# Diagonal score tiles packed by quarters, nine exponential fills per unit in place of ten, and keys turned from a buffer

## The chip, the cores and the metric

The kernel runs on one core of a Trainium2 chip. The core has a matrix engine (TensorE, PE in the profile), whose weight loads are listed apart as PEld, a vector engine (VectorE, DVE), an engine for activation functions (ScalarE, ACT), GpSimd (POOL) and SyncE (SP), which here issues nearly all DMAs. The metric is device time in microseconds (us); the median of several timed executions counts.

## The reference

The output has two halves side by side, 640 columns each, for 2048 tokens.

Half A is a convolution over the whole sequence. Keys are filtered with four short taps per channel, multiplied by the values, convolved with a filter of 2048 taps per channel (an FFT in the reference), and multiplied by the queries:

```
kv = k_shift * v
y  = irfft(rfft(kv padded) * rfft(ssm_k padded))[:2048] + kv * ssm_D
a  = q * y
```

Half B is attention with 32 heads of 20 channels, in four segments of 512 tokens. In a segment each token attends causally to tokens of the same segment (softmax), and to earlier segments through a memory matrix that is summed up from segment to segment:

```
p     = softmax(q k^T * scale + mask);  a_dot = p v
a_mem = phi(q) M / (phi(q) z + 1e-6)
o     = g * a_mem + (1 - g) * a_dot;  b = o wo
M    += phi(k)^T v;  z += sum phi(k);   phi(t) = t + 1 where t > 0, else exp(t)
```

## The kernel before

Half A is cut into five blocks of 128 channels (`conv(dp)`, dp 0 to 4). The long convolution is a transform done by matmuls with a constant matrix (`spectrum`), a product of spectra on VectorE (`product`), and matmuls back (`inverse`). The short filter (`short_filter`) is done by matmuls, too: the keys lie turned, channels on partitions, in `kr`, each eighth token is taken as weights, and diagonal matrices of taps (`skd`) are streamed through. For dp in `TAP2` (2, 3 and 4) pairs of taps are joined: half of the partitions hold keys shifted by two tokens, copied by three DMAs between `kr` and `kb`, so that fewer columns are streamed. The keys come to `kr` by one transposing DMA from memory.

Half B has eight units: four segments, each with two halves of 16 heads (`project(u)` and `attend(u)`, u from 0 to 7). `project` multiplies the segment's turned input `xT` by the weights, evicts keys, queries and values to SBUF, turns keys and queries by DMA into `KQT`, takes the positive feature map (`phi`), bounds the scores (`bound`, whose rows are written into spare rows of the turned queries by four small DMAs), and adds this segment to the memory `Mbd`.

`attend` treats the 16 heads in four groups of four. A head has 20 channels on 32 partitions, so the four heads of a group lie on the four quarters of the array's rows, and their matmuls stand side by side. Scores are made transposed: keys on partitions, queries along the columns. A segment of 512 tokens has four token tiles of 128; of the 4 x 4 blocks of scores the ten at and below the diagonal are needed. They are put into *fills*. A fill is four PSUM banks, one per head, of 512 columns each, and two exponentials (ACT, 128 x 1024 each) that carry it to an SBUF buffer `ET`. Per group there is one fill A (keys of tile 0 with queries of tiles 1 to 3, and keys of tile 2 with queries of tile 3) and one fill D (the four diagonal blocks). Per two groups there is one fill J (keys of tile 1 with queries of tiles 2 and 3, for both groups). This makes ten fills and twenty exponentials per unit. In a fill D the mask is put into PSUM first: 16 matmuls of constant matrices (`pack` in the profile), then 16 of keys and queries.

`values` then multiplies the exponentials, as weights, by the values with a column of ones (21 columns), 40 matmuls per group, and beside them four matmuls with the memory for later segments. VectorE takes reciprocals, scales, adds the two parts and writes `o_s`. `project_out` turns `o_s` and multiplies it by `wo`.

All operations are recorded first (`Recorder`), and a list of numbers worked out beforehand (`ORDER`) says in which order they are issued, engine by engine; another (`BASE`) gives each group of results its PSUM banks. So all instructions carry the line of the issuing helper, L256, and the profile is read by tiles and shapes. The string `EVICT` says for each of 238 evictions whether VectorE (1) or ScalarE (0) does it. SP's queue is served in order: a DMA whose source is not ready holds up those behind it. Warming matmuls (`WARM`, tile `o` in the profile) run at the start.

## Time and profile before

| What | Value |
|---|---|
| Median of three timed runs | 272.57 us (272.38 to 272.6) |
| Profiled execution: span from the first to the last instruction | 272.0 us |
| Time outside that span, median less span | about 0.6 us |
| PE busy, instructions | 260.8 us, 4368 |
| PE weight loads busy, instructions | 195.4 us, 4371 |
| DVE busy, instructions | 250.9 us, 424 |
| ACT busy, instructions | 248.8 us, 388 |
| DMA, queue of SP | 42.91 MB, 79.9% of 16 engines' time |

The profiled execution's own time was not taken apart from its span; the timed median stands beside it. The table's busy times are unions: where two instructions of an engine overlap, the time counts once. PE instructions are listed with a modelled end and overlap strongly, so for PE the distance between starts is what an instruction costs. A shape like `32*128 32x384` means weights of 32 rows by 128 columns, and an input of 32 rows by 384 columns streamed through them. In a row of groups the numbers are: busy us, mean ns of one, idle time before them and who ended it. A row of the timeline has start, length, engine, operation, shapes and count of instructions that follow each other; a row of waits has total us, times, longest.

### The profile page before, as it was taken

To read this page: it belongs to the slowest core of one execution; us is meant where nothing else is said; L and a number is where in the kernel's file an instruction comes from. 1 tells how busy PE (TensorE), PEld (TensorE's weight loads), DVE (VectorE), ACT (ScalarE), POOL (GpSimd) and SP (SyncE) were. 2 spreads that over 40 slices of the span, in tenths; PEclk is the share of its full clock that TensorE was granted. 3 is DMA by queue.
4 is the path that set the end of the run, shared out by engine and by line. 5 is a ranking of instruction groups with operands and counts; after the bars stand their busy time and mean duration, and the time that the engine had idled before them with its cause. 6 is when DMAs were issued, how large, how long until landed. Compare 5 with 4: busy or idle time off the path is not lost.

```text
span 272.0 us, 10130 instructions
## 1 busy us (share of the span) xinstructions
PE 260.8 (96%) x4368; PEld 195.4 (72%) x4371; DVE 250.9 (92%) x424; ACT 248.8 (91%) x388; POOL 6.9 (3%) x18
## 2 busy tenths in 40 slices
PE   8999999999998999999999999999999989999995
PEld 3879777868766677878676787768677765756783
DVE  0599999999999999999999999999999998999972
ACT  1586799999999999999999999999999998999962
POOL 9100000000000000000000000000000000000000
PEclk9999999999999999999999999999999997999999
DMA  6999399999989599998979599994974081894024
GB/s 166 347 207 243 82 191 225 311 194 172 170 217 201 144 195 195 191 178 159 159 165 190 116 151 226 147 197 65 146 177 82 4 154 27 169 155 90 27 68 133
DMA packets 126972, 43.74 MB, mean 161 GB/s; under 512 B 117339, under 2 KB 124512, under 8 KB 126800
## 3 DMA queue, kind: packets, MB, share of 16 engines
q1 hardware_dynamic: 126768, 42.91, 79.9%
q8 instruction: 34, 0.56, 0.9%
q0 software_dynamic: 160, 0.20, 0.2%
q14 instruction: 10, 0.08, 0.1%
HBM read 14.12 MB, written 7.34 MB: 79 GB/s over the span
## 4 chain that ended last, share of the span: by engine, by line
PE 55%; ACT 33%; issue 6%; DVE 4%; ACTq 0%; DVEq 0%
PE ps L256 55%; ACT ET L256 21%; ACT F L256 4%; ACT KQ L256 3%; ACT PP L256 3%; ACT outb L256 1%; ACT Va L256 1%; DVE F L256 1%; DVE pq L256 1%; DVE Kh L256 1%; ACT bT L256 1%; DVE qabs L256 0%; DVE vt L256 0%; DVE Xh L256 0%; DVE PP L256 0%
## 5 line engine op out<-in xcount | busy, mean ns | idle before, releaser
L256 ACT ACTIVATE ET<-ps 128x1024 bf16<-128x1024 f32 x160 | 160.6, 1102 | 1.9 <-PE ps L256 1.7
L256 PE MATMUL ps<-wqkv,xT 128*128 128x320 bf16 x480 | 76.3, 300 | 0.5 <-ACT ET L256 0.3
L256 PEld LDWEIGHTS <-xT 128*128 128x128 bf16 x640 | 58.1, 98 | 25.7 <-issue 5.2
L256 PE MATMUL ps<-Va,ET 128*128 128x21 bf16 x1280 | 42.4, 172 | 0.3 <-ACT ET L256 0.3
L256 ACT CAST F<-ps 128x512 bf16<-128x512 f32 x69 | 42.0, 687 | 0.3 <-PE ps L256 0.3
L256 PEld LDWEIGHTS <-ET 128*128 128x128 bf16 x1280 | 39.7, 96 | 3.0 <-issue 2.2
L256 PE MATMUL ps<-KQT 32*128 32x128 bf16 (+2 forms) x896 | 34.6, 240 | 1.1 <-ACT ET L256 1.0
L256 PEld LDWEIGHTS <-Wf 128*128 128x128 bf16 x320 | 28.9, 97 | 6.1 <-issue 1.5
L256 ACT CAST KQ<-ps 128x320 bf16<-128x320 f32 x61 | 28.2, 496 | 1.4 <-PE ps L256 1.3
L256 PE MATMUL ps<-wo,xT 128*128 128x320 bf16 x160 | 25.4, 299 | 0.0
L256 PEld LDWEIGHTS <-KQT 32*128 32x128 bf16 x896 | 16.0, 92 | 10.9 <-issue 9.9
L256 PE MATMUL ps<-vt,Wf 128*128 128x256 bf16 x160 | 22.4, 272 | 0.1
L256 PE MATMUL ps<-kT,Wf 128*128 128x256 bf16 x160 | 22.2, 273 | 0.2 <-ACT ET L256 0.2
L256 PE MATMUL ps<-Y,Wi 128*128 128x256 bf16 x160 | 21.7, 280 | 0.0
L256 DVE TENSOR_TENSOR o<-ps,rr 128x640 bf16<-128x640 f32 x24 | 19.5, 814 | 0.2
L256 PE MATMUL ps<-Mbd,PqT 128*128 128x84 bf16 x96 | 18.1, 202 | 1.2 <-ACT ET L256 0.9
L256 DVE TENSOR_TENSOR Y<-Y,pq 128x2048 bf16<-128x2048 bf16 (+1 forms) x20 | 18.6, 945 | 0.0
L256 DVE TENSOR_TENSOR pq<-Xh,Kh 128x2048 bf16<-128x2048 bf16 x15 | 18.1, 1209 | 0.0
L256 PEld LDWEIGHTS <-Wi 128*128 128x128 bf16 x160 | 15.3, 100 | 3.5 <-issue 1.0
L256 ACT ACTIVATE PP<-KQ 128x640 bf16<-128x640 bf16 (+1 forms) x18 | 17.7, 991 | 0.0
L256 PE MATMUL ps<-pack 32*128 32x128 bf16 x512 | 14.7, 216 | 1.9 <-ACT ET L256 1.7
L256 ACT CAST Va<-ps 128x320 bf16<-128x320 f32 x31 | 15.0, 520 | 1.2 <-PE ps L256 1.2
(93 smaller groups left out, 370.0 us busy)
## 6 DMA issues: line engine op xcount, KB each, us to landing
vt<-in_A_v_dram SPq DMA_DIRECT2D x10, 256.0 KB
pq<-in_A_q_dram SPq DMA_DIRECT2D x10, 256.0 KB
out_dram<-outb SPq DMA_DIRECT2D x13, 160.0 KB
turned<-kT SPq DMA_DIRECT2D x4, 512.0 KB
kT<-turned SPq DMA_DIRECT2D x8, 256.0 KB
out_dram<-pq SPq DMA_DIRECT2D x8, 256.0 KB
kb<-kr SPq DMA_DIRECT2D x6, 256.0 KB
Wf<-c_wf SPq DMA_DIRECT2D x4, 256.0 KB
```

Of the source, the lines that this page charges most:

```text
L256: f(*[fix(a) for a in args], **{k: fix(v) for k, v in kw.items()})
```

## The change

The diagonal blocks are packed closer. Of a diagonal block of 128 x 128 one quarter (later keys, earlier queries) is masked altogether, so three quarters of it are kept. Token tiles 2 and 3 are held with their halves of 64 tokens exchanged, from the load of `x` on (five transposing DMAs in place of one, and an exchanged identity in segment 0), until the output is written (two stores of 64 rows in place of one for tiles 2 and 3) or turned back in the last segment. With that, the small quarter (64 keys, 64 queries) of a tile 2 or 3 lies on partitions 64 to 127 and that of tile 0 or 1 on partitions 0 to 63, and a pair of diagonal blocks takes 192 columns instead of 256. Two pairs take 384, and the 128 columns left in a fill D take the block of keys 1 and queries 2. What was left in J (keys 1, queries 3) is one block per group, and one J per unit holds it for all four groups, in a buffer of its own (`EJ`). So a unit has four fills A, four D and one J.

In a D fill there are now 24 mask matmuls of 64 columns; sixteen score matmuls of 64 columns with 128-column weights, sixteen with 64-column weights that go to one half of the partitions, and four of 128 columns, in two rounds of the loop over `P`. The diagonal's value matmuls become an operation of its own (`OD`): per group 16 matmuls with weights of 64 rows by 128 columns, then 16 with 64 rows by 64 columns, the two of a pair on opposite rows and into different banks. The other 24 value matmuls per group stay. In segment 0 the two groups of a pair share one set of banks and one division.

Beside that: the keys of dp 1 to 4 are loaded in token rows into `kb` (two DMAs), turned from there into `kr` (two transposing DMAs) so that the tokens taken together lie side by side, and copied by five DMAs; dp 1 joins those with paired taps. The tap matrices of dp 0 and 1 are made at the start (`filter_weights`). The memory's old state is added in PSUM by a matmul with the identity, where two VectorE steps did it before. `phi` of the queries is done once for four token tiles, not twice for two. The column of ones stands ahead of the values in place of behind them, with a second one for the memory. `A` of the bounds has 4 columns in place of 32. There are 10 warming matmuls for 20, six `ET` buffers for seven, a new `ORDER` and `BASE`, and an `EVICT` with 26 ones of 238 in place of 31. `KSW` and `IW` are all 1, so they join nothing.

```diff
+    def filter_weights(self, dp):
+        V = self.nc.vector
+        self.rec.key = ("skd", dp)
+        if dp in TAP2:
+            w = self.ring("skd", [128, 2, 2, 64], n=1)
+            V.tensor_tensor(out=w[:], in0=self.id2[:, None, None, :].to_broadcast([128, 2, 2, 64]),
+                            in1=self.taps[:, 0:4, dp].rearrange("p (f l) -> p f l", f=2)[:, :, :, None].to_broadcast([128, 2, 2, 64]), op=ALU.mult)
+        else:
+            w = self.ring("pq", [128, 4, 4, 128], n=PQBUF)[:, 0]
+            V.tensor_tensor(out=w, in0=self.ident[:, None, :].to_broadcast([128, 4, 128]), in1=self.taps[:, 4:8, dp, None].to_broadcast([128, 4, 128]), op=ALU.mult)
+        self.skd[dp] = w
...
+                    rows = flat[:, 1024 * a:1024 * a + 1024]
+                    nc.sync.dma_start(out=rows.rearrange("p (e d) -> p e d", e=8), in_=self.k[1024 * a:1024 * a + 1024, dsl].rearrange("(p e) d -> p e d", e=8))
+                for a in range(2):
+                    key("kx", a)
+                    nc.sync.dma_start_transpose(out=kr[:, :, KPAD + 128 * a:KPAD + 128 * a + 128], in_=flat[:, 1024 * a:1024 * a + 1024])
                 key("lc")
                 q = self.queue("lc", dp)
-                q.dma_start(out=self.kb[64:128, KPAD:KPAD + S], in_=kr[64:128, KPAD:KPAD + S])
-                q.dma_start(out=self.kb[0:64, KPAD:KPAD + S], in_=kr[64:128, KPAD - 2:KPAD + S - 2])
-                q.dma_start(out=kr[64:128, KPAD:KPAD + S], in_=kr[0:64, KPAD - 2:KPAD + S - 2])
+                q.dma_start(out=kb[64:128], in_=kr[64:128])
+                q.dma_start(out=kb[0:64, 2:8], in_=kr[64:128, 0:6])
+                q.dma_start(out=kb[0:64, 0:2, KPAD - 1:], in_=kr[64:128, 6:8, KPAD - 2:-1])
+                q.dma_start(out=kr[64:128, 2:8], in_=kr[0:64, 0:6])
+                q.dma_start(out=kr[64:128, 0:2, KPAD:], in_=kr[0:64, 6:8, KPAD - 1:-1])
+            else:
+                nc.sync.dma_start_transpose(out=flat[:, KPAD:KPAD + S], in_=self.k[:, dsl])
...
-            nc.sync.dma_start_transpose(out=xT[:], in_=self.x[L * s:L * s + L, :])
+            for to, n, at in ((0, 256, 0), (256, 64, 320), (320, 64, 256), (384, 64, 448), (448, 64, 384)):
+                nc.sync.dma_start_transpose(out=xT[:, :, to:to + n], in_=self.x[L * s + at:L * s + at + n, :])
...
+                        nc.tensor.matmul(pmv[:, k, :, 1:VW], lhsT=PP[:, 0, t, 4 * k:4 * k + 4, :], rhs=Va[:, t, 4 * k:4 * k + 4, 1:VW],
+                                         start=(k == 0 and t == 0), stop=False, grp=g, skip_group_check=True)
+                nc.tensor.matmul(pmv[:, :, :, 1:VW], lhsT=self.ident[:], rhs=src[:, :, :, 1:VW], start=False, stop=True, grp=g, skip_group_check=True)
+            V.tensor_tensor(out=dst[:, :, :, 1:VW], in0=pmv[:, :, :, 1:VW], in1=self.maskbd[:, None, :, 1:VW].to_broadcast([128, 4, 4, DH + 1]), op=ALU.mult, grp=g)
...
+            ET = self.ring("EJ", [128, 4, 4, 128])[:].rearrange("p h g q -> p h (g q)") if kind == "J" else self.ring("ET", [128, 4, 512], n=ETBUF)
...
         def diagonal(gg):
+
             def parts(heads):
-                for i in range(4):
-                    for hl, bank, r, g in heads:
-                        nc.tensor.matmul(bank.rearrange("p (b q) -> p b q", b=4)[:, :, 32 * i:32 * i + 32], lhsT=self.mleft[r, i, :],
-                                         rhs=self.mright[r, None, :].to_broadcast([32, 4, 32]), start=(i == 0), stop=False, grp=g, skip_group_check=True)
-                for kc in range(4):
-                    for hl, bank, r, g in heads:
-                        block(bank[:, 128 * kc:128 * kc + 128], hl, gg, kc, 128 * kc, 128, start=False, stop=(kc == 3), grp=g)
+                for i in range(2):
+                    for at, m0 in ((64, 64), (128, 0), (0, 128)):
+                        for hl, bank, r, g in heads:
+                            nc.tensor.matmul(bank[:, 0:384].rearrange("p (b q) -> p b q", b=2)[:, :, at + 32 * i:at + 32 * i + 32], lhsT=self.mleft[r, i, m0:m0 + 128],
+                                             rhs=self.mright[r, None, :].to_broadcast([32, 2, 32]), start=(i == 0 and at == 64), stop=False, grp=g, skip_group_check=True)
+                for P in range(2):
+                    a, b = 128 * P, 128 * P + 256
+                    for at, k, q in ((128, a, a + 64), (0, b, b)):
+                        for hl, bank, r, g in heads:
+                            nc.tensor.matmul(bank[:, 192 * P + at:192 * P + at + 64], lhsT=KT[r, gg, k:k + 128], rhs=QT[r, gg, q:q + 64], start=False, stop=False, grp=g, skip_group_check=True)
+                    for to, k, q in ((0, a, a), (64, b + 64, b + 64)):
+                        for hl, bank, r, g in heads:
+                            nc.tensor.matmul(bank[to:to + 64, 192 * P + 64:192 * P + 128], lhsT=KT[r, gg, k:k + 64], rhs=QT[r, gg, q:q + 64], start=False, stop=False, grp=g, skip_group_check=True)
+                for hl, bank, r, g in heads:
+                    block(bank[:, 384:512], hl, gg, 1, 256, 128, start=False, stop=True, grp=g)
             return parts
...
-        def joined(g0):
-            def parts(heads):
-                for k in range(2):
-                    for hl, bank, r, g in heads:
-                        block(bank[:, 256 * k:256 * k + 256], hl, g0 + k, 1, 256, 256, start=True, stop=True, grp=g)
-            return parts
...
+        def joined(heads):
+            for k in range(4):
+                for hl, bank, r, g in heads:
+                    block(bank[:, 128 * k:128 * k + 128], hl, k, 1, 384, 128, start=True, stop=True, grp=g)
+
+        def weighted(gg, Dg, Bg, J, g, j):
+            if s:
+                sums = g.ap[:, :, 0:352].rearrange("p b (k c h e) -> p b k c h e", k=2, c=2, h=4)
+                dots, mems = sums[:, :, 0], sums[:, :, 1]
+            else:
+                dots = g.ap[:, :, 0:352].rearrange("p b (c k h e) -> p b c k h e", k=2, c=2, h=4)[:, :, :, j]
+            up, low = slice(0, 64), slice(64, 128)
+            rec.key = ("OD", u, gg)
+            with rec.one():
+                for late in range(2):
+                    for P in range(2):
+                        a, b = 192 * P + 64, 192 * P
+                        for hl in range(4):
+                            if late:
+                                todo = [(0, low, low, Dg[low, hl, a + 64:a + 128]), (1, up, up, Dg[up, hl, b:b + 64])]
+                            else:
+                                todo = [(0, up, slice(0, 128), Dg[up, hl, a:a + 128]), (1, low, slice(0, 128), Dg[low, hl, b:b + 128])]
+                            for odd, rows, to, e in todo:
+                                nc.tensor.matmul(dots[to, odd, P, hl, 0:DH + 1], lhsT=e, rhs=Va[rows, P + 2 * odd, 4 * gg + hl, 0:DH + 1],
+                                                 start=(not late and P == 0 and hl == 0 and j == 0), stop=False, grp=g, skip_group_check=True)
...
+                        for q in (0, 1) if qc == 1 else (qc,):
+                            nc.tensor.matmul(mems[:, q // 2, q % 2, :, 1:VW], lhsT=PqT[:, q, gg, :], rhs=Mbd[:, gg, :, 1:VW], start=False, stop=False, grp=g, skip_group_check=True)
                     for hl in range(4):
+                        blocks = [(0, Bg[:, hl, 128 * (qc - 1):128 * qc])]
+                        blocks += [(1, Dg[:, hl, 384:512] if qc == 2 else J[:, hl, 128 * gg:128 * gg + 128])] if qc > 1 else []
+                        blocks += [(2, Bg[:, hl, 384:512])] if qc > 2 else []
+                        for kc, e in blocks:
+                            nc.tensor.matmul(dots[:, qc // 2, qc % 2, hl, 0:DH + 1], lhsT=e, rhs=Va[:, kc, 4 * gg + hl, 0:DH + 1], start=False, stop=True, grp=g, skip_group_check=True)
...
+        J = fill("J", ("J",), joined)
         for pp in range(2):
             g0 = 2 * pp
-            A0 = fill("A", (g0, "A"), 235, below(g0))
-            D0 = fill("D", (g0, "D"), 456, diagonal(g0))
-            J = fill("J", (g0, "J"), 235, joined(g0))
-            A1 = fill("A", (g0 + 1, "A"), 235, below(g0 + 1))
-            D1 = fill("D", (g0 + 1, "D"), 456, diagonal(g0 + 1))
-            values(g0, D0, A0, J)
-            values(g0 + 1, D1, A1, J)
+            parts = []
+            for gg in (g0, g0 + 1):
+                Dg = fill("D", (gg, "D"), diagonal(gg))
+                Bg = fill("A", (gg, "A"), below(gg))
+                parts.append((Dg, Bg))
+            values(pp, parts)
...
-FBUF, ETBUF, PQBUF = 1, 7, 1
-WARM, WARMC = 20, 512
+FBUF, ETBUF, PQBUF = 1, 6, 1
+WARM, WARMC = 10, 512
...
-TAP2 = (2, 3, 4)
+TAP2 = (1, 2, 3, 4)
...
```

More of the change, by code (lines that the diff above doesn't have):

```diff
@@ L280, in __init__ @@
         self.real = tc.nc
[L281 removed]
+        self.rings, self.skd = {}, {}
         self.evicts = 0
@@ L344, in __init__ @@
         self.evict(self.taps[:], tp, g)
+        for dp in range(2):
+            self.filter_weights(dp)
         rec.key = ("zero",)
@@ L643, in project @@
             tok = slice(128 * t, 128 * t + 128)
+            rows = [xT[:, cc, tok] for cc in range(5)]
             rec.key = ("P", u, t)
@@ L649, in project @@
                         for cc in range(5):
-                            nc.tensor.matmul(g.ap[:, i, 0:320], lhsT=xT[:, cc, tok], rhs=self.wqkv[:, cc, half, i0 + i, :], start=(cc == 0), stop=(cc == 4), grp=g)
+                            nc.tensor.matmul(g.ap[:, i, 0:320], lhsT=rows[cc], rhs=self.wqkv[:, cc, half, i0 + i, :], start=(cc == 0), stop=(cc == 4), grp=g)
                 self.evict(KQ[:, t, i0:i0 + KQW, :, 0:DH], g.ap[:, :, 0:320].rearrange("p i (h d) -> p i h d", d=DH), g)
@@ L849, in project_out @@
             rec.key = ("OB", s, t)
-            self.stores(last).dma_start(out=self.out[L * s + 128 * t:L * s + 128 * t + 128, D:2 * D], in_=outb.rearrange("p a b -> p (a b)"))
-FBUF, ETBUF, PQBUF = 1, 7, 1
-WARM, WARMC = 20, 512
+            rows = self.out[L * s + 128 * t:L * s + 128 * t + 128, D:2 * D]
+            flat = outb.rearrange("p a b -> p (a b)")
+            for x, y in ((0, 64), (64, 0)) if t > 1 and not last else ((0, 0),):
+                n = 128 if x == y else 64
+                self.stores(last).dma_start(out=rows[x:x + n], in_=flat[y:y + n])
+FBUF, ETBUF, PQBUF = 1, 6, 1
+WARM, WARMC = 10, 512
 TURN = (0,)
```

245 lines of the change are left out of this document (114 added, 131 removed).

## The prediction

> **What bounds the kernel now.** I read the page first, then the groups of instructions with shapes kept apart, then the timeline of TensorE (PE) and last the waits.
>
> ```profile
> span 272.0 us, 10130 instructions
> PE 260.8 (96%) x4368; PEld 195.4 (72%) x4371; DVE 250.9 (92%) x424; ACT 248.8 (91%) x388; POOL 6.9 (3%) x18
> PE 55%; ACT 33%; issue 6%; DVE 4%; ACTq 0%; DVEq 0%
> PE ps L256 <- ACT ET L256: 5.2, 15, 0.7
> ```
>
> Three engines are busy over 90% of the span, and the chain of waits runs through PE for 55% and ACT for 33%. Matmuls overlap, so 260.8 says little of what PE has left. The distance from one start to the next says it. The fence holds rows of PE's timeline: start, length, shape, count.
>
> ```profile
> 42.66 1.10 PE L256 MATMUL ps<-skd,kr 128*128 128x512 bf16 x7
> 43.60 1.52 PE L256 MATMUL ps<-wqkv,xT 128*128 128x320 bf16 x10
> ...
> 116.27 0.39 PE L256 MATMUL ps<-ident,kmx 128*128 128x128 bf16 x4
> 116.59 0.40 PE L256 MATMUL ps<-pack 32*128 32x128 bf16 x16
> 116.82 0.39 PE L256 MATMUL ps<-KQT 32*128 32x128 bf16 x16
> 117.15 0.28 PE L256 MATMUL ps<-skd,kr 128*128 128x128 bf16 x1
> ...
> 120.54 0.85 PE L256 MATMUL ps<-wqkv,xT 128*128 128x320 bf16 x5
> 121.32 0.40 PE L256 MATMUL ps<-KQT 32*128 32x384 bf16 x8
> 121.65 0.85 PE L256 MATMUL ps<-wqkv,xT 128*128 128x320 bf16 x5
> 122.34 0.22 PE L256 MATMUL ps<-skd,kr 128*128 128x128 bf16 x1
> ...
> 122.93 0.84 PE L256 MATMUL ps<-wqkv,xT 128*128 128x320 bf16 x5
> ...
> 125.67 1.04 PE L256 MATMUL ps<-vt,Wf 128*128 128x256 bf16 x8
> 126.54 0.20 PE L256 MATMUL ps<-Mbd,PqT 128*128 128x84 bf16 x1
> 126.58 0.25 PE L256 MATMUL ps<-Va,ET 128*128 128x21 bf16 x4
> ...
> 127.30 0.55 PE L256 MATMUL ps<-Va,ET 128*128 128x21 bf16 x16
> 127.71 0.20 PE L256 MATMUL ps<-Mbd,PqT 128*128 128x84 bf16 x1
> ```
>
> Five projections take 122.34 - 121.65 = 0.69 when another 128-row matmul follows, 0.137 each, but 121.32 - 120.54 = 0.78 when a 32-row fill follows: going to 32 rows costs 0.10. Fill A (8 matmuls, four heads side by side, 512 columns a head) holds PE for 0.33, of which 512/320 x 0.137 = 0.22 is streaming, so the way back costs 0.11. Fill D takes 0.23 for masks, 0.33 for scores, 0.10 to enter: 0.66. A round of four heads with 128 columns is 0.23/4 = 0.057. Sixteen value matmuls take 127.71 - 127.30 = 0.41, 0.026 each; eight of 256 columns 0.87, 0.109 each; an 84-column one 0.04. One convolution tile takes 0.94 with full taps (dp 0 and 1), 122.93 - 122.34 = 0.59 with paired taps.
>
> Counts come from the groups, two of which stand here, and from the loops of the code (160 output projections, three times 160 matmuls of 256 columns, 80 fills, 32 of them D). PE's work without waits:
>
> ```profile
> L256 PE MATMUL ps<-wqkv,xT 128*128 128x320 bf16 x480 | 76.3, 300 | 0.5 <-ACT ET L256 0.3
> L256 PE MATMUL ps<-Va,ET 128*128 128x21 bf16 x1280 | 42.4, 172 | 0.3 <-ACT ET L256 0.3
> ```
>
> (480 + 160) x 0.137 = 87.7; 1280 x 0.026 = 32.8; 480 of 256 columns x 0.109 = 52.3; 48 fills A and J x 0.43 = 20.6; 32 fills D x 0.66 = 21.1; 192 of 84 columns x 0.04 = 7.7; convolution 8 x 0.94 + 12 x 0.59 = 14.6; 120 turning matmuls x 0.057 = 6.8; bounds 8 x 0.44 = 3.5; warming about 7. Together 254. PE starts at 1.3 and 3.4 us pass after its last matmul, so of 272.0 only some 13 us are waits, 5.2 of them for the exponentials. **PE's own work is a bound, as tight as ACT and DVE.**
>
> **The change, part by part.** The sum is against the span of 272.0; the timed median of 272.57 lies 0.6 above it.
>
> ACT. Nine fills of two exponentials in each of 8 units are 144 for 160.
>
> ```profile
> 227.45 5.61 ACT L256 ACTIVATE ET<-ps 128x1024 bf16<-128x1024 f32 x6 [1.34 <-PE ps L256]
> L256 ACT ACTIVATE ET<-ps 128x1024 bf16<-128x1024 f32 x160 | 160.6, 1102 | 1.9 <-PE ps L256 1.7
> L256 ACT CAST KQ<-ps 128x320 bf16<-128x320 f32 x61 | 28.2, 496 | 1.4 <-PE ps L256 1.3
> L256 DVE TENSOR_TENSOR mt<-mt,em 128x16 bf16<-128x16 bf16 x6 | 1.3, 212 | 0.0
> L256 DVE TENSOR_TENSOR Mbd<-Mbd,mt 128x336 bf16<-128x336 bf16 x6 | 2.0, 325 | 0.0
> L256 DVE TENSOR_TENSOR PP<-PP,qabs 128x640 bf16<-128x640 bf16 x12 | 5.7, 474 | 0.0
> L256 DVE TENSOR_TENSOR PP<-PP,qabs 128x1280 bf16<-128x1280 bf16 x6 | 4.9, 816 | 0.0
> ```
>
> Six in a row step by (5.61 - 1.10)/5 = 0.90, so 16 fewer free 14.4 us. The string of evictions has 26 on DVE for 31: five go to ACT, at most 0.5 each, 2 us. With the merged phi (half as many, twice as long, some 1 us less) ACT falls by 13 to 236.
>
> DVE loses those five (about 2.5), the two memory steps at 0.212 and 0.325 six times (3.2), half the phi steps (5.7 to 4.9, and as much again for its companion, 1.6), and a little where segment 0 treats two head groups in one step (1): some 8 us, to 243.
>
> PE, the fills. J goes from 16 to 8, each still 0.43 (four rounds of 0.057, 0.10 in, 0.11 out): -3.4. D becomes six mask rounds of 64 columns, four score rounds of 64 columns into 128 partitions, four into 64 partitions, one of 128 columns. No row shows 32-row rounds of 64 columns; half of 0.057 is the floor, 0.029, and 0.057 the ceiling. I take 0.029, since value matmuls of 21 columns reach 0.026 with a full weight load each. The rounds into 64 partitions have one relative in the trace, the filter's turning at the start. It loads 64 columns of weights into the two halves in turn and then 128 columns. The rows come from short stretches of the timeline, one ending just after the first pair, one after the fourth, one further on; the last row is of the groups:
>
> ```profile
> 9.19 0.22 PE L256 MATMUL ps<-ident,skd 5*64 5x5 bf16 x2
> ...
> 9.19 0.40 PE L256 MATMUL ps<-ident,skd 5*64 5x5 bf16 x8
> ...
> 9.53 0.25 PE L256 MATMUL ps<-ident,skd 5*128 5x5 bf16 x3
> L256 PE MATMUL ps<-ident,skd 5*64 5x5 bf16 x8 | 0.4, 201 | 0.0
> ```
>
> From two matmuls to eight the group grows by 0.18: pairs follow each other every 0.06, though they stream five columns. The last pair starts near 9.59 - 0.20 = 9.39 and the first 128-column one at 9.53: 0.13, about 0.10 beyond the floor of 0.026. **So going from 64 to 128 columns of the array costs what going to 32 rows does.** D's loop over the two pairs of tiles goes to 64 and back twice, four switches of 0.10 inside each fill. D is then 0.10 + 10 x 0.029 + 2 x 0.06 (the rounds for both halves together) + 4 x 0.10 + 0.057 + 0.11 = 1.08, 0.42 more, 32 times: +13.4. If the switches cost nothing it is +0.6; with rounds at 0.057 it is +22.
>
> The Trainium skill, TensorEngine Tiling (Array Packing), Key Properties, says that changing the tiling mode, not only the tile, drains TensorE; the 0.10 and 0.11 of the fills agree, and the sum by the rule is the one above.
>
> PE, the values. The sixteen diagonal matmuls of a head group (0.41) become 32: eight pairs on 64 rows, then eight pairs on 64 rows and 64 columns. The two of a pair use other rows and other banks, so I count a pair once: 8 x 0.026 for the first set, and for the second between 0.026 (a value matmul) and 0.06 (the turning above, whose weights were read in strides). I take the middle, 0.043. Three switches (into 64 rows, to 64 columns, back) add 0.30. That is 0.84, 0.43 more, 32 times: +13.8, with ends +9 and +18. Where the new order puts the set next to a fill one switch is shared; I take that everywhere, -3.2.
>
> On the weights' price the Trainium skill, TensorE: Matmul & The Clock Gate, Weight-path perf modes, says that the fast load needs 128 columns. With its plain rate, columns over 1.2 per ns, 64 columns are an estimated 53 ns and the sum is 2.6 us more.
>
> PE, the rest. dp 1 goes to paired taps, 4 x (0.94 - 0.59) = -1.4; keys that lie in a row instead of every eighth should load at the streaming pace, 6 x 0.057 + 4 x 0.029 = 0.46 for 0.59 on 16 tiles, -2.1 (0 if strides were not the cause). The memory's sum by an identity matmul of 336 columns is 6 x 0.14 = +0.8. Ten warming matmuls fewer save nothing, as PE then waits for the same first load:
>
> ```profile
> 1.26 6.16 PE L256 MATMUL ps<-o 128*128 128x512 bf16 x18 [1.26 <-DVE o L256]
> ...
> 7.25 0.66 PE L256 MATMUL ps<-ident,kT 128*128 128x128 bf16 x8
> ```
>
> Net for PE: -3.4 + 13.4 + 13.8 - 3.2 - 3.5 + 0.8 = +18.
>
> Queues. Each paired dp turns its keys from the buffer kb: two loads, two transposes and five copies where dp 2 to 4 had one transpose and three copies.
>
> ```profile
> 81.63 3.42 SPq L256 DMA_TRANSPOSE kr<-in_A_k_dram  x1
> 94.75 1.39 SPq L256 DMA_TRANSPOSE KQT<-KQ  x1
> 97.48 1.31 SPq L256 DMA_DIRECT2D kb<-kr  x2
> SPq L256 <- PE ps L256: 45.1, 19, 9.2
> ```
>
> At 1.39 a transpose of 256 KB and 0.65 a copy that is 7.3 us of issue for 5.4, and 7.3 for 3.4 on dp 1; twelve more transposes of x in small pieces (same bytes) and six more stores add under 10. Behind them in SP's queue stand the turned KQ and the bound rows, for which the fills wait. SP now waits 45.1 us for PE alone, so some 20 us more of issue fit; bounds 0 and +5, taken 0.
>
> Buffers. D and B of a pair of head groups hold four of six buffers until their values ran, and J has its own, so a third pair's fill can start; before, two pairs shared seven. I take 0; if a fill had to wait for values, a round of 0.8 each would be the price of one wait.
>
> **Sum.** PE 254 + 18 = 272 of work, 4.7 at the two ends, and 3 of the 13 us of waits: those for ACT and DVE shrink, as both now have 25 us to spare, those for the first loads stay. Span 279.6, time 280. With 13 us of waits 290, with the cheap values and no waits 272.
>
> **The rivals.**
> Faster, by relief of ACT and DVE: the 64-wide tiles run beside the 128-wide ones without a drain. Then D costs +0.6, the values 0, and PE falls by 6 to 248. DVE decides: 243 of work and the 21 us in which it was not busy (272.0 - 250.9) give 264; between 260 and 269 with the sharing of evictions. For it speaks that PE waits for ACT, 5.2 us; against it the 0.13 at 9.4 us. It decides if D fills come out under 0.75 and the value sets near 0.45.
> No change: value sets at the cheap end (+9), nothing waits any more; 267 + 4.7 = 272.
> Much slower: rounds of 64 columns held at 0.057 by weight loads (+9) and SP's longer queue bringing keys or rows late (+5): 290 to 298. Each of 72 fills would start late after a transpose.
> That fewer exponentials run is fixed by the counts, so the change does at least that.
>
> **How the numbers follow.** Forecast 280 (274 to 290) 0.49; faster, 264, 0.33; no change 0.10, split 0.04, 0.05, 0.01; much slower 0.08. A measurement here can tell 0.2%, 0.5 us. Faster 0.37, same 0.05, slower 0.58. The range 262 to 290 leaves out under 2 in 10: the lower half of the fast case and most of the slowest.
>
> **What would show it.** Right: D fills near 1.1 from first mask to next start, 0.13 gaps between 64- and 128-column rounds, value sets near 0.8, PE without waits while ACT and DVE show holes, exponentials x144. Wrong: 64-column rounds 0.03 after 128-column ones, ACT and DVE still full at a shorter span; or SP's transposes ending the waits of fills.

## The result, and the profile after

The changed kernel takes 305.19 us (median of four runs, 301.92 to 305.9) where the kernel before takes 272.56. By the means of the runs that is 1.117 times as long, with a 95% interval of 1.111 to 1.123. The forecast was 280, range 262 to 290; the direction was right and the size was not. Medians here leave out a run more than 1.5% above the fastest of its kernel (there is one each in `keys_before`, `regroup`, `before_narrow`, `lean_replan2` and `after_pool`), while the expectations' gains of 2.8 us for `keys_before` and 4.8 for `regroup` have it counted. The profiled execution, the slowest of the four, shows a span of 304.1 us. From its page come the span, the busy times, the granted clock in 40 slices and the chain by engine:

```profile
span 304.1 us, 12942 instructions
PE 281.7 (93%) x5786; PEld 207.9 (68%) x5787; DVE 249.9 (82%) x385; ACT 242.4 (80%) x371; POOL 7.2 (2%) x18
...
PEclk9999997999999599999999999999599999979999
...
PE 58%; DMA 17%; SPq 11%; DVE 6%; ACT 3%; issue 3%; DVEq 0%; ACTq 0%
```

Two numbers divide the 32.1 us of span. PE is busy 281.7 us for 260.8 (+20.9), and the time in which it is not busy goes from 272.0 - 260.8 = 11.2 to 304.1 - 281.7 = 22.4 us (+11.2). The chain of waits, in which ACT had 33% before, now has 28% of DMAs and SP's queue, and ACT 3%.

The relief of ScalarE came as counted (two rows: its exponentials, by groups, and what PE waits for, with total, times and longest):

```profile
L257 ACT ACTIVATE ET<-ps 128x1024 bf16<-128x1024 f32 x128 | 126.6, 1038 | 17.0 <-PE ps L257 15.4
```

```profile
PE ps L257 <- DMA kr<-kr: 2.5, 3, 0.9
PE ps L257 <- issue: 2.5, 3, 1.3
PE ps L257 <- DMA xT<-in_B_x_dram: 2.2, 2, 1.4
PE ps L257 <- ACT KQ L257: 1.9, 1, 1.9
PE ps L257 <- DMA KQT<-bT: 1.3, 1, 1.3
...
PE ps L257 <- DVE o_s L257: 1.2, 1, 1.2
...
PE ps L257 <- ACT ET L257: 0.2, 1, 0.2
```

With 16 in `EJ` there are 144 exponentials. PE waits 0.2 us for them (5.2 before); it is ACT that waits, 15.4 us. PE's new waits are for keys, inputs, bound rows and evictions, many small ones at many places; for 2.5 us of them ("issue") the profile shows no releaser.

PE's timeline shows what the new fills and value sets cost (start, length, shape, count):

```profile
108.13 0.35 PE L257 MATMUL ps<-pack 32*128 32x64 bf16 x24
108.32 0.89 PE L257 MATMUL ps<-KQT 32*128 32x64 bf16 x36
109.14 0.85 PE L257 MATMUL ps<-wqkv,xT 128*128 128x320 bf16 x5
...
115.94 0.71 PE L257 MATMUL ps<-Va,ET 64*128 64x21 bf16 x32
116.58 1.05 PE L257 MATMUL ps<-Y,Wi 128*128 128x256 bf16 x8
```

Six mask rounds take 0.19 us, 0.032 each. A D fill takes 109.14 - 108.13 = 1.01 from its first mask to the next work, a set of 32 value matmuls 116.58 - 115.94 = 0.64. The like in the kernel before is 117.15 - 116.59 = 0.56 (the prediction's 0.66 has 0.10 in it for entering the fill, which the 1.01 has not) and 0.41. That is 32 x 0.45 = 14.4 and 32 x 0.23 = 7.4 us; with the prediction's -3.4 for J, -3.5 for the filter and +0.8 for the memory, **PE's own work grew by 15.7 us**. Entering the value sets is not in this; where a set follows work on 128 rows it is about 0.08 each, at most 2 us over all. Most of the other 5 of the 20.9 is not work: see the clock.

**One wait followed through.** Views of DVE, SP and PE between 87 and 99 us, then stretches of 2 us with the granted clock as the number right behind POOL's count:

```profile
95.24 1.23 DVE L257 TENSOR_TENSOR pq<-Xh,Kh 128x2048 bf16<-128x2048 bf16 x1 [2.19 <-DMA out_dram<-pq]
...
98.03 0.82 DVE L257 TENSOR_TENSOR o_s<-ps,rr 128x640 bf16<-128x640 f32 x1
```

```profile
87.03 2.08 SPq L257 DMA_TRANSPOSE kT<-in_A_ssm_k_dram  x1
89.21 0.61 SPq L257 DMA_DIRECT2D kb<-in_A_k_dram  x1
89.86 0.67 SPq L257 DMA_DIRECT2D out_dram<-pq  x1
```

In the kernel before, SP issues the two stores of the same buffer together:

```profile
73.76 1.39 SPq L256 DMA_DIRECT2D out_dram<-pq  x2
```

PE after, and the stretches:

```profile
97.38 0.33 PE L257 MATMUL ps<-KQT 32*128 32x384 bf16 x2
98.90 0.39 PE L257 MATMUL ps<-KQT 32*128 32x384 bf16 x6 [1.19 <-DVE o_s L257]
```

```profile
97.00:99.00 2.00, 0.81 (x10) 0.29 (x9) 1.97 (x4) 1.47 (x3) 0.00 (x0) 1.00 1.03 344
99.00:101.00 2.00, 2.00 (x52) 1.44 (x49) 1.97 (x3) 1.65 (x2) 0.00 (x0) 0.80 1.68 178
101.00:103.00 2.00, 2.00 (x26) 1.54 (x26) 1.93 (x3) 0.53 (x2) 0.00 (x0) 0.50 0.38 81
103.00:105.00 2.00, 2.00 (x49) 1.30 (x48) 1.97 (x2) 1.36 (x3) 0.00 (x0) 0.50 1.32 66
105.00:107.00 2.00, 2.00 (x27) 1.42 (x26) 0.38 (x2) 1.47 (x3) 0.00 (x0) 0.50 1.02 226
```

The finished convolution output is stored from `pq`, of which there is one buffer, and VectorE's next product goes into `pq`. The last write of the output in question ended at 81.56. Its first half is stored at 84.08, the second at 89.86, behind a transposed filter and a load of keys; VectorE waits 2.19 us for it. In the kernel before both stores stand ahead of the filter and the keys, and VectorE's product at 82.39 does not wait. Behind the product in VectorE's order stands the division `o_s`, which empties a PSUM bank that a fill A needs: PE gets two of eight matmuls out and waits 1.19 us. And then PE runs at half clock for 6.8 us, though it is busy again. One late store costs PE 1.2 us by the wait and, if the clock fell because of that wait, up to 3.4 by the clock.

Rows of 40 us give the clock over the span, after first, then before; in the rows left out PE works at 1.00:

```profile
40.00:80.00 40.00, 37.09 (x786) 28.50 (x785) 33.27 (x51) 33.06 (x51) 0.00 (x0) 0.96 0.93 194
80.00:120.00 40.00, 38.81 (x831) 28.23 (x816) 33.94 (x44) 33.89 (x53) 0.00 (x0) 0.91 1.06 182
...
200.00:240.00 40.00, 37.22 (x775) 26.46 (x775) 31.89 (x48) 32.23 (x51) 0.00 (x0) 0.91 0.60 121
240.00:280.00 40.00, 38.27 (x993) 27.66 (x993) 34.72 (x54) 35.33 (x51) 0.00 (x0) 0.96 0.43 87
```

```profile
200.00:240.00 40.00, 37.58 (x759) 27.49 (x758) 38.38 (x67) 38.66 (x55) 0.00 (x0) 0.96 0.52 95
```

40 x (0.04 + 0.09 + 0.09 + 0.04) = 10.4 us of clock are missing after, 1.6 before. The difference, 8.8 us, is the most that the clock can have cost. The kernel before shows what it does cost: of its 11 runs beside `after_replan`, five have a whole clock (mean 272.6 us) and six have 0.992 or 0.993, as with the one stretch of 3.4 us at half in its profile (mean 273.5). If these runs differ in nothing else, a stretch costs 0.8 us. The changed kernel's 20.5 us at half are six such lengths for one before, an estimated 4 us more. Together: 15.7 of work and 11.2 of waits leave 5.2 of the 32.1 us for the clock and for entering the value sets.

### The profile page after: what moved, and what is told of

Its sections match the earlier page's. It is cut to its first block, busy times and chain, and to the rows that moved or that the text cites. A ratio compares the mean times of both kernels' runs of the same rounds, so it can differ in the third digit from the quotient of the medians.

```text
span 304.1 us, 12942 instructions
## 1 busy us (share of the span) xinstructions
PE 281.7 (93%) x5786; PEld 207.9 (68%) x5787; DVE 249.9 (82%) x385; ACT 242.4 (80%) x371; POOL 7.2 (2%) x18
## 4 chain that ended last, share of the span: by engine, by line
PE 58%; DMA 17%; SPq 11%; DVE 6%; ACT 3%; issue 3%; DVEq 0%; ACTq 0%
PE ps L257 58%; SPq L257 11%; DMA kT<-in_A_ssm_k_dram 2%; DMA PqT<-PP 2%; DMA Y<-in_B_x_dram 2%; DMA out_dram<-pq 2%; DMA kr<-kr 2%; DMA kb<-kr 2%; DMA KQT<-KQ 2%; ACT ET L257 2%; DMA kr<-kb 2%; DVE Kh L257 1%; DMA KQT<-bT 1%; DMA pq<-in_A_q_dram 1%; DVE o L257 1%
## 5 line engine op out<-in xcount | busy, mean ns | idle before, releaser
L257 ACT ACTIVATE ET<-ps 128x1024 bf16<-128x1024 f32 x128 | 126.6, 1038 | 17.0 <-PE ps L257 15.4
L257 PE MATMUL ps<-Va,ET 64*128 64x21 bf16 (+2 forms) x1664 | 52.6, 175 | 2.3 <-issue 2.2
L257 PEld LDWEIGHTS <-ET 64*128 64x128 bf16 (+2 forms) x1664 | 46.6, 101 | 10.3 <-issue 7.5
L257 PE MATMUL ps<-KQT 32*64 32x64 bf16 (+3 forms) x1536 | 46.5, 219 | 2.5 <-DMA KQT<-bT 1.3
L257 PEld LDWEIGHTS <-KQT 32*128 32x128 bf16 (+1 forms) x1536 | 25.4, 95 | 17.2 <-issue 10.9
L257 DVE RECIPROCAL rr<-ps 128x32 f32<-128x32 f32 x28 | 9.9, 354 | 13.2 <-PE ps L257 13.0
L257 PE MATMUL ps<-Y,Wi 128*128 128x256 bf16 x160 | 20.5, 273 | 0.0
L257 DVE TENSOR_TENSOR pq<-Xh,Kh 128x2048 bf16<-128x2048 bf16 x15 | 18.2, 1215 | 2.3 <-DMA out_dram<-pq 2.2
L257 DVE TENSOR_TENSOR vt<-ps,vt 128x512 bf16<-128x512 f32 x20 | 13.1, 684 | 5.7 <-ACT ET L257 2.4
L257 ACT ACTIVATE PP<-KQ 128x1280 bf16<-128x1280 bf16 x12 | 15.3, 1288 | 2.9 <-DMA PqT<-PP 2.8
L257 ACT ACTIVATE EJ<-ps 128x1024 bf16<-128x1024 f32 x16 | 16.1, 1040 | 1.4 <-PE ps L257 1.4
L257 DVE TENSOR_TENSOR pq<-ps,pq 128x512 bf16<-128x512 f32 x20 | 13.5, 685 | 4.5 <-DMA pq<-in_A_q_dram 2.8
## 6 DMA issues: line engine op xcount, KB each, us to landing
kb<-kr SPq DMA_DIRECT2D x4, 272.0 KB
```

Source lines behind the costliest of these rows:

```text
L257: f(*[fix(a) for a in args], **{k: fix(v) for k, v in kw.items()})
```

## Experiments

Three theories: (1) the added DMAs make SP's queue late; (2) PE's own narrow rounds and their switches hold the time; (3) the new written order puts instructions where the chip has their sources late. Medians are given beside the ratio to the kernel before, whose median was 272.7 to 273.1 in these runs. Where the edit removes or adds operations, the written order of the others is kept, but for a few that must stand behind what they read (a projection of unit 2 where x comes whole, a copy where keys do).

### Parts of the change undone

`x_whole` (in this run and in `x_whole_keys_before`, one projection result of unit 2 also comes into a PSUM bank before a spectrum was read from it, which changes that part of the output too):

```diff
-            for to, n, at in ((0, 256, 0), (256, 64, 320), (320, 64, 256), (384, 64, 448), (448, 64, 384)):
-                nc.sync.dma_start_transpose(out=xT[:, :, to:to + n], in_=self.x[L * s + at:L * s + at + n, :])
+            nc.sync.dma_start_transpose(out=xT[:], in_=self.x[L * s:L * s + L, :])
```

> The changed kernel, but x of segments 1 to 3 comes in one transposing DMA each instead of five. Left out: the half-exchange of the tokens there, so the scores of two of four token tiles are of other tokens. Theory 1 (SP's queue is late, and what it brings ends PE's waits): SP issues 12 DMAs and some 17 us less (its x rows 28.3 us x15 in the changed kernel, 10.8 us x3 before), PE's waits of 39 us fall by about 10, time 293 to 298. Theory 2 (TensorE's own rounds and switches in the new fills): none of them changes, time 303 to 307. Theory 3 (the order as it is written out): also 303 to 307.

Measured 302.42 us, 1.107 (1.103 to 1.112).

`keys_before`:

```diff
-                    nc.sync.dma_start(out=rows.rearrange("p (e d) -> p e d", e=8), in_=self.k[1024 * a:1024 * a + 1024, dsl].rearrange("(p e) d -> p e d", e=8))
...
+                nc.sync.dma_start_transpose(out=krf[:, KPAD:KPAD + S], in_=self.k[:, dsl])
...
+                q.dma_start(out=flat[64:128, KPAD:KPAD + S], in_=krf[64:128, KPAD:KPAD + S])
+                q.dma_start(out=flat[0:64, KPAD:KPAD + S], in_=krf[64:128, KPAD - 2:KPAD + S - 2])
+                q.dma_start(out=krf[64:128, KPAD:KPAD + S], in_=krf[0:64, KPAD - 2:KPAD + S - 2])
```

> The changed kernel with the old way of the keys for pairs 1 to 4: one transposing DMA from memory and three copies, read with a stride of 8. The output is the reference's. Theory 1 (SP's queue): SP issues some 17 us less (keys 40.5 us of issue against 23 before), and the waits that end on kr, kb and the keys from memory (4.69 and 6.84 us are the largest) go; time 290 to 298. Theory 2 (TensorE's rounds): the strided reading comes back, up to 2 us more, 304 to 307. Theory 3 (the order): 303 to 307.

Measured 300.34 us, 1.105 (1.097 to 1.114). By the medians the two gain 2.8 and 4.9 us, by the means 2.3 and 2.9, where theory 1 wanted 7 to 15. The runs of one kernel lie 3 to 4 us apart, so that neither gain alone is clear of the noise.

`x_whole_keys_before`, both edits:

> Both at once: x whole in segments 1 to 3 (tokens not exchanged there) and the old way of the keys. Theory 1: SP's issue is back at about 192 us (193.9 before the change, 226.5 after), PE's waits fall from 39 to about 20, time 282 to 288. Theory 2: 303 to 307. If one half of the effect of SP hides behind the other, this is less than the sum of the two single runs.

Measured 300.79 us, 1.101 (1.096 to 1.106). Theory 1 in this form falls: with the DMAs of x and keys as before, 4.4 us are gained where 17 to 23 were expected. VectorE and SP of this run show why:

```profile
97.77 1.23 DVE L257 TENSOR_TENSOR pq<-Xh,Kh 128x2048 bf16<-128x2048 bf16 x1 [4.03 <-DMA out_dram<-pq]
```

```profile
88.52 2.55 SPq L257 DMA_TRANSPOSE kT<-in_A_ssm_k_dram  x1
91.18 2.90 SPq L257 DMA_TRANSPOSE kr<-in_A_k_dram  x1
94.12 0.60 SPq L257 DMA_DIRECT2D out_dram<-pq  x1
```

The same store is even later, since the whole transposed load of keys (2.90) now stands ahead of it. Fewer DMAs in the same order leave this fault of the order in place.

`wide`:

```diff
-                            nc.tensor.matmul(bank[to:to + 64, 192 * P + 64:192 * P + 128], lhsT=KT[r, gg, k:k + 64], rhs=QT[r, gg, q:q + 64], start=False, stop=False, grp=g, skip_group_check=True)
+                            nc.tensor.matmul(bank[:, 192 * P + 64:192 * P + 128], lhsT=KT[r, gg, (a, b)[to // 64]:(a, b)[to // 64] + 128], rhs=QT[r, gg, q:q + 64], start=False, stop=False, grp=g, skip_group_check=True)
...
+                        for odd, e in ((0, Dg[:, hl, a:a + 128]), (1, Dg[:, hl, b:b + 128])):
+                            nc.tensor.matmul(dots[:, odd, P, hl, 0:DH + 1], lhsT=e, rhs=Va[:, P + 2 * odd, 4 * gg + hl, 0:DH + 1],
```

> The changed kernel without its narrow weights: the D fill's rounds with 64 weight columns get 128, the value products of the diagonal become 16 matmuls of full 128 x 128 weights per group. The same exponentials, DMAs and written order; the scores of the narrow blocks are overwritten by wider ones and the output is not the reference's. Theory 2 (narrow rounds and mode switches): four switches of .07 to .12 us and the switch at 64 rows go from 32 fills and value sets, 13 to 16 us less TensorE work, time 288 to 293. Theory 1 (SP's queue sets the pace): PE gets its work done sooner and waits the more, 301 to 305.

Measured 296.41 us, 1.083 (1.079 to 1.088): between the theories. The page:

```profile
span 295.9 us, 11918 instructions
PE 263.5 (89%) x5274; PEld 198.2 (67%) x5275; DVE 248.9 (84%) x385; ACT 239.1 (81%) x371; POOL 7.2 (2%) x18
```

PE is busy 18.2 us less and idle 295.9 - 263.5 = 32.4, which is 10 more: half of what is taken off PE comes back as waits. So PE's work is a part of the cause, and something stands behind it.

`wide_x_keys`, the three edits together:

> Three parts undone at once: no narrow weights in the D fills and the diagonal values (as in the run wide), x whole in segments 1 to 3, the old way of the keys. Left out: scores of the narrow blocks are overwritten and the tokens of segments 1 to 3 are not exchanged, so the output is not the reference's. If the 8.8 us of the narrow weights and the 4.4 us of the DMAs are separate costs they add up: 291 to 293. If one hides the other: 295 to 297. If the rest of the 32 us stood behind both together (a DMA that comes late only because PE is late): 280 or less.

Measured 287.5 us, 1.052 (1.046 to 1.058): 17.7 us off, where `wide` (8.8) and `x_whole_keys_before` (4.4) add to 13.2. The parts may hide each other a little, and 15 us remain.

`regroup`:

```diff
+                for hl, bank, r, g in heads:
+                    block(bank[:, 384:512], hl, gg, 1, 256, 128, start=False, stop=False, grp=g)
+                for P in range(2):
+                    a, b = 128 * P, 128 * P + 256
                     for to, k, q in ((0, a, a), (64, b + 64, b + 64)):
...
-                for hl, bank, r, g in heads:
-                    block(bank[:, 384:512], hl, gg, 1, 256, 128, start=False, stop=True, grp=g)
```

> The changed kernel, with the rounds of the D fill put in another order: the mask, all score rounds with 128 weight columns of both pairs, the block of 128 queries, and then all rounds with 64 weight columns. One change to 64 columns instead of two there and two back inside a fill; the same products, the output is the reference's. Theory 2 (mode switches): three switches of .07 to .12 us fewer in 32 fills, D 0.2 to 0.3 us shorter, 7 to 10 us less TensorE work and as much off the time, 294 to 299. Theory 3 (order and late DMAs): PE has the time as waits instead, 302 to 305.

Measured 299.51 us, 1.096 (1.091 to 1.102), 5.7 off (5.2 by the means). PE's timeline:

```profile
109.71 0.35 PE L257 MATMUL ps<-pack 32*128 32x64 bf16 x24
109.90 0.55 PE L257 MATMUL ps<-KQT 32*128 32x64 bf16 x36
110.38 0.85 PE L257 MATMUL ps<-wqkv,xT 128*128 128x320 bf16 x5
```

D takes 0.67 for 1.01 with the same 60 matmuls: three switches fewer and narrow rounds side by side save 0.34, 11 us over 32 fills. What is left above the 0.56 of before is 0.11, about one switch. **What made D long was the switches, not the narrow rounds**, and half of the saving shows in the time.

### One part alone in the kernel before

`before_x5`:

```diff
-            nc.sync.dma_start_transpose(out=xT[:], in_=self.x[L * s:L * s + L, :])
+            for to, n in ((0, 256), (256, 64), (320, 64), (384, 64), (448, 64)):
+                nc.sync.dma_start_transpose(out=xT[:, :, to:to + n], in_=self.x[L * s + to:L * s + to + n, :])
```

> The kernel before, with x of segments 1 to 3 loaded by five transposing DMAs each of the same tokens in the same order. The output is the reference's. Theory 1 (SP's one queue is full through the first 220 us, in the kernel before too, so that every us put into it is a us later for what stands behind): 17 us more of issue, time 277 to 286. If SP has room, as the prediction took it: 272 to 274.

Measured 276.48 us, 1.014 (1.011 to 1.016), 3.4 more, just under what theory 1 wanted. SP had no room for 12 transposes at nothing. PE waits for `xT<-in_B_x_dram`, as in the changed kernel, and for `xT<-o_s`:

```profile
PE ps L256 <- DMA xT<-o_s: 1.7, 1, 1.7
...
PE ps L256 <- DMA xT<-in_B_x_dram: 0.6, 1, 0.6
```

`before_narrow`:

```diff
+                    if kc == 1:
+                        for to in (0, 64):
+                            for hl, bank, r, g in heads:
+                                nc.tensor.matmul(bank[to:to + 64, 128:256], lhsT=KT[r, gg, 128 + to:192 + to], rhs=QT[r, gg, 128:256], start=False, stop=False, grp=g, skip_group_check=True)
+                        continue
```

> The kernel before with one of the four score rounds of each D fill (keys and queries of token tile 1) made with 64 weight columns, for the upper and the lower half of the partitions in turn, between rounds with 128 columns: two changes of the array's columns in each of 32 fills, the same products, order, DMAs and exponentials. The output is the reference's. By the changed kernel's trace a change is 0.11 us and the second half round 0.03 to 0.06, so TensorE has 8 to 9 us more work. If TensorE's work is the bound in the kernel before: 278 to 282. If its waits take it up: 272.5 to 275.

Measured 279.21 us, 1.019 (1.016 to 1.023), 4 to 6 more. PE's timeline, a D fill up to the next other work:

```profile
117.53 0.40 PE L256 MATMUL ps<-pack 32*128 32x128 bf16 x16
117.76 0.64 PE L256 MATMUL ps<-KQT 32*128 32x128 bf16 x20
118.33 0.28 PE L256 MATMUL ps<-skd,kr 128*128 128x128 bf16 x1
```

0.80 for the 0.56 of the kernel before (116.59 to 117.15) is 0.24 more, 7.7 us over 32 fills, and more than half of it is in the time. PE's work was a bound indeed, though not one for one.

### The order alone

For these, an order was searched in which every operation, with the lengths, delays and landings that the traces show, ends early. In `after_replan`, `before_replan` and `after_replan2` only the string `ORDER` differs.

`after_replan` and its control `before_replan`:

> The changed kernel with another written order and nothing else: the same instructions, DMAs and PSUM banks, moved so that the starts, the lengths and the landings read from the traces of the runs so far fit each other, SP's DMAs included. The output is the reference's. Counted by distances between starts, TensorE's own work is 249 us before the change and 266 after it. Theory 3 (the new order puts DMAs and evictions where the chip has them late, and TensorE's waits follow from that): the waits of 39 us fall to under 20 and the time to 278 to 286. Theory 2 (TensorE's own rounds hold the time): no order helps by more than a few us, 299 or more. Theory 1 in its strict form (SP issues too much): between, 292 to 300, since nothing is issued less.

> The control of the new order: the kernel before with its order worked over in the same manner and with the same lengths, nothing else. The output is the reference's. If the order of before already fits the chip: 269 to 273, so that the gain of the changed kernel by the same treatment belongs to its own order. If the treatment helps any order alike: 255 to 262.

`after_replan` took 292.16 us, 1.073 (1.068 to 1.078): 13.0 us off with the same instructions (11.5 by the means). `before_replan` took 284.27, 1.039 (1.035 to 1.043): the same treatment *loses* 11.2 us on the order of before. It is a poor planner, and still it improves the changed kernel's order by 13. Theory 2 alone can't be; the strong form of theory 3 (278 to 286) was not reached. From `after_replan`'s page, of its slowest execution (295.93):

```profile
span 294.2 us, 12939 instructions
PE 276.7 (94%) x5786; PEld 205.9 (70%) x5787; DVE 253.7 (86%) x385; ACT 241.6 (82%) x371; POOL 7.1 (2%) x18
```

PE is idle 17.5 us for 22.4, and busy 5 us less with the same matmuls and less of its time at half clock (mean clock 0.988 for 0.966).

`after_replan2`:

> The changed kernel with a second new written order. The first one had moved early loads so that PE waited 4.4 us for the identity and 2.3 us for beta at the start; here the first 14 us stay as they were, and the order is fitted to lengths with some scatter added. The output is the reference's. Theory 3: the 6 us of the start come off what the first one measured (292.2), 284 to 289. Theory 2 (what is left is TensorE's own work): 291 to 295 again.

Measured 296.85 us, 1.087 (1.083 to 1.091): a miss. The start was mended, and other waits came. Its page gives the work another way, since PE's clock was nearly whole (0.994 over the span):

```profile
span 294.7 us, 12943 instructions
PE 275.8 (94%) x5787; PEld 204.8 (70%) x5787; DVE 253.2 (86%) x385; ACT 242.0 (82%) x371; POOL 7.2 (2%) x18
```

275.8 less 0.006 x 275.8 = 1.7 is 274.1; before, 260.8 less 1.6 is 259.2. By this the work grew by 14.9, where the rows gave 15.7. (The expectations' count by distances between starts, 249 and 266, made it 17.) I keep 15 to 17.

`lean_replan` and `lean_replan2`, which join `regroup`, `keys_before` and two fitted orders:

> The changed kernel with three repairs: the D fill's rounds regrouped (one change to 64 columns), the keys in the old way, and an order fitted in the second manner. The output is the reference's. TensorE's work is then some 253 us (249 before the change, 266 after it). If the parts add (regrouped 4.8 us, keys 2.8, order 13 to 18): 280 to 285, still slower than the kernel before. If the narrow rounds and the late DMAs only showed because the order was tight against them: 272 to 279.

> The changed kernel with regrouped D rounds and the old way of the keys, as in lean_replan (283.2), with a second fitted order. The output is the reference's. TensorE's work is 253 us by distances between starts and some 24 us of waits were left in lean_replan. If the order can still give: 274 to 281. If TensorE's work and its ends are the floor: 281 to 285. Below 272.6 it would beat the kernel before; the sum says it does not.

Measured 283.17 us, 1.038 (1.031 to 1.045), and 282.52, 1.032 (1.028 to 1.037). No version beat the kernel before. The page of `lean_replan`, with the clock whole:

```profile
span 281.9 us, 12924 instructions
PE 265.6 (94%) x5787; PEld 201.6 (72%) x5787; DVE 250.4 (89%) x385; ACT 239.8 (85%) x371; POOL 7.2 (3%) x18
...
PEclk9999999999999999999999999999999999999999
```

PE's work is 265.6 - 259.2 = 6.4 us above that of before, its idle time 16.3 for 11.2, 5.1 more. These 11.5, less the 1.6 of clock that the kernel before is charged with here, are the 9.9 by which the spans differ.

`wide_x_keys_replan`:

> As wide_x_keys (no narrow weights, x whole in segments 1 to 3, the old way of the keys; narrow scores overwritten and tokens not exchanged, so the output is not the reference's), with an order fitted to the lengths in the traces, the first 14 us kept. If the 15 us that wide_x_keys (287.5) has over the kernel before are the order's: 271 to 276. If they belong to something else in the change: 283 or more.

Measured 280.55 us, 1.026 (1.024 to 1.029), 7 of the 15 us; between the two expectations. That is 3.7 less than `before_replan`, but not by the same treatment: here the first 14 us were kept, while in `before_replan` PE waits 3.3 us for its first load where the kernel before waits 1.3. Whether what is left of the change is slower than the kernel before under one treatment is not shown, nor how low a good order would go.

### Another queue

`after_pool`:

```diff
-BULK = ()
+BULK = ("lv", "lq")
...
-STQ = 1
+STQ = 0
```

> The changed kernel with its 42 stores and loads of values and queries issued by GpSimd, whose queue stands empty, in place of SP; the bytes and the written order stay. The output is the reference's. Theory 1a (SP's queue, where one DMA that waits for its source holds up those behind it): SP issues some 30 us less, time 290 to 296. Theory 1b (the 16 DMA engines are full for the first 220 us, so that bytes and small packets count and not the queue they come by): 301 to 306. Theory 2 and 3: 301 to 306.

Measured 315.63 us, 1.154 (1.150 to 1.159). Both readings of theory 1 are missed: moved to GpSimd, these DMAs make the kernel 10 us slower. Whether GpSimd's issuing or the shared DMA engines is to blame was not separated.

## Why the prediction was wrong

**What held.** PE's own work was a bound (`before_narrow`). 144 exponentials, ACT and DVE full of holes, and PE's waits for exponentials gone: right. D near 1.1: 1.01, or 1.11 with the 0.10 for entering that the sum's 1.08 has in it. Rounds of 64 columns near the floor of 0.029: 0.032. Switches between 64 and 128 columns near 0.10: three of them and the joined narrow rounds are worth 0.34 in `regroup`. The Trainium skill, TensorEngine Tiling (Array Packing), Key Properties, which lets a change of the tiling mode drain TensorE, agrees with that 0.34.

**Sizes that were off.** The value set came out at 0.64, or about 0.72 with entering, not 0.84: +7.4 us, up to +9 with entering, for the +10.6 (13.8 - 3.2) of the sum. (Redone, the 0.84 is 0.85 and the cheap end 9.8, not 9; neither matters here.) D gave +14.4 for +13.4. The net for PE's work was 15 to 17 for 18: nearly right, and by this alone the kernel would have come out close to the forecast. SP's issue grew by more than was counted: 193.9 to 226.5 us, 32.6 more, where the prediction has under 20. The parts of x alone went from 10.8 to 28.3, where they and six stores were to add under 10.

**The step that failed** is in the sum: "and 3 of the 13 us of waits". The forecast was 18 of work less 10 of waits; the span shows some 16 of work, 11 of waits and 5 of clock, so the waits alone are off by 21 us and the clock, which had no term, by 5. The waits for ACT shrank as argued, but waits are not a stock that only shrinks. PE's idle time doubled, 11.2 to 22.4, with other releasers in place of the old one: DMAs, and divisions held up by DMAs. Two earlier terms feed into it. SP's longer queue was "taken 0" between bounds 0 and +5; x alone costs 3.4 us in the old order, x and keys 4.4 in the new one. And the new order had no term at all. The prediction walked the queues for the DMAs that were added, not for those that were moved, like the store of `pq` behind a filter load, and it took for granted that the new order waits as little as the old one. Another order alone gives back 13 us (`after_replan`). One of the prediction's own signs of being wrong came true: DMAs of SP end waits of PE.

**What was not thought of** is the clock. PE ran at half clock for 20.5 us, an estimated 4 to 5 us' worth more than before and at most 8.8, and only where it had waited shortly before. Every term of waits should have been dearer by that.

The rival "much slower" had the right second half (keys and rows late), the wrong first half (rounds at 0.057), and at 290 to 298 still missed the time.

**What stays open.** The work (15 to 17) and the waits (11.2) are read from the profile; the clock's 4 to 5 is what they leave, and the estimate from the runs of the kernel before is near it. How the waits divide between the added DMAs and the order is not settled: undoing x and keys in the given order gains 4.4, the order alone 13.0, and the two overlap. No run undoes the six `ET` buffers, the `EVICT` string or the shorter warming, which came with the change. Under equal treatment the changed kernel is 292.16 - 284.27 = 7.9 us slower; whether that is the change's own price under a good order was not shown, since no order found here was as good for the kernel before as its own.

## What to carry to other kernels

A change that comes with a rewritten order has to be costed as two changes: walk each in-order queue for what now stands ahead of a buffer's release (a store that frees the only copy of a buffer first of all), and give "the order fits worse" a term of its own in the sum. Here three engines were above 90%, and the relief of two of them did not become slack for the third; it became waits at other places. And group rounds by the array's columns: putting all narrow rounds last in a fill cut a third of it with the same products.

## What the hardware showed unexpectedly

PE's granted clock fell to 0.50 for 3.4 or 6.8 us, starting 0.8 to 2.3 us after PE had stood still for 0.9 to 1.9 us (once in two waits close together); the rows from 97 to 107 us show one after a wait of 1.19. In the changed kernel there were four such stretches, in `lean_replan` none. The kernel before has one of 3.4 us, at 224 us, after waits of 0.39 and 0.69 for the exponentials. Not every wait does it: with the same two waits at 225 us `before_x5` kept its clock whole. The stretches from 133 to 139 us of the changed kernel, too, hold waits of 1.37 (from 132.84 on) and 0.93, with the clock whole:

```profile
133.00:135.00 2.00, 0.79 (x9) 0.44 (x9) 1.52 (x3) 0.65 (x3) 0.00 (x0) 1.00 0.64 119
135.00:137.00 2.00, 1.07 (x21) 0.56 (x21) 1.59 (x3) 1.92 (x4) 0.00 (x0) 1.00 0.79 188
137.00:139.00 2.00, 2.00 (x29) 1.43 (x26) 1.19 (x2) 1.27 (x2) 0.00 (x0) 1.00 1.03 220
```

The Trainium skill, TensorE: Matmul & The Clock Gate, part 1, has the clock halve after an idle window of about 3.4 us that runs freely, and come back after one busy window. The length of the dips agrees with that window, and a free-running window would explain that of two like waits only one is punished. That a whole window must be idle does not agree: 1.19 us of waiting was enough here.
